# Attention and a gated FFN on one core: where the end keeps its rows of x and gates, and which engine copies and combines at a block change

## The chip, the core and the metric

The kernel runs on one core of a Trainium2 chip. A core has a matmul engine (TensorE, PE in the profile, with its weight loads listed as PEld), VectorE (DVE), ScalarE (ACT), GpSimd (POOL) and SyncE (SP), whose queue issues all the transfers here. Each engine works through its own queue in order; semaphores tie the queues together. [...] The metric is the device time of one execution in microseconds (us); the median of the runs counts.

## The reference

All in fp32, with S = 2048 tokens, D = 576, 32 heads of 18 and F = 4608:

```
xn = layernorm(x)
q, k, v = split(xn @ wqkv)                      # 32 heads of 18
s = softmax(q k^T / sqrt(18)) v  @ wo           # attention block
g = silu( (gelu(xn @ w_gate) * (xn @ w_up)) @ w_down )
out = x + s * g
```

`gelu` is the tanh form. Both branches read the same normalised x; the two results meet in the last line.

## The kernel before

**Tiling.** Tokens come in NB = 4 blocks of TB = 512, the hidden width in 36 slices of 128 for each block, so there are NF = 144 FFN sections. A section n is 27 pairs of matmuls for gate and up (lines 413 to 430, rows `L427`): the 576 input features are nine chunks of 64, and each chunk is multiplied three times, since every fp32 operand is cut into a high part in fp32r and a low part (`wh`, `wl` for the weights, two tiles per chunk group for x). The gate runs on partitions 0 to 63 of the array and up on 64 to 127, so x must lie in both halves: `load_xd` brings it to the lower half and `copy_xd` copies it to the upper, part 0 (high) on ScalarE (`L151`) and part 1 (low) on GpSimd (`L153`). With every new block x is exchanged in this way (`new` in `section`).

After the section `activate` makes the hidden slice h, `sums_a` and `cut_a` build from it the operands `ah` and `al` on GpSimd (`L455`, `L456`, `L462` to `L467`), and every second section `down` multiplies them with the down weights T: 42 matmuls in seven products (`py`, `L538`), each added by VectorE into the accumulator M (`L542`), or copied into it by ScalarE for the first slice of a block (`L540`). The seven products stand for eight (a scheme with sums of sub-blocks), so at the end of a block M's seven parts are combined into four (`combine`, `L553`; the list `COMBINED` gives four times one step on VectorE and one on GpSimd), and `gates` stores the four quarters to `ys` in DRAM.

**Attention** runs between the pairs of the sections. NU = 32 units (a block of queries, four heads) take four sections each; each section has eight slots, a slot being a score pair (`pe`, `L825`, then exp on ScalarE, `L826`) and a maximum pair (`pm`, `L774`, then a reduction on VectorE, `L776`) for the unit after. Values are `acc` (`L842`). When the maxima of a unit are complete, `max_parts` negates them (VectorE), cuts them in two on GpSimd (`L789`, `L790`), turns them on VectorE (`max_turn`, `L795`) and sends them over DRAM (`max_store`, `max_end`) into rows of QT, where the scores of the next unit read them. The last three are hooked between pairs of the following section: pairs 4, 5 and 16.

**Order.** PE and SP follow the program. ScalarE, VectorE and GpSimd are ordered by the framework's planner until the last part, except where an instruction is marked with `keep`: that pins it behind the instruction that the program gives the same engine just before. Hooks (`FF["hooks"]`) name the pair of the next section at which a step is written. In the last part (lines 1063 to 1117) all engines follow the program. Transfers use eight semaphores in turn, and a request waits for the one eight before it.

**The end.** Five gate/up sections are left when attention is over, with three down products. Between them stand 16 groups of 128 tokens, each a `step()`: `split_o` cuts the group's attention output (in KA) into `oh` (ScalarE `L948`, VectorE `L950`) and `ol` (VectorE `L949`); `project_o` multiplies it with wo in 28 matmuls (`po`, `L974`); `gate` makes silu of the stored gate rows by a tanh on ScalarE (`L964`) and a product on VectorE (`L965`); VectorE multiplies this with `po` (`L981`); GpSimd adds x (`L988`; VectorE for the last block), and the group is stored (`L1004`). `load_xy` (`L957`) asks for the rows of x and gates: four x tiles, three gate tiles, two groups ahead. The store of a group is requested one step later than its sum, behind the requests of that step. The cut of a group is queued one group ahead. Scaling the last attention rows (`scale`, `L700`), the loads of gate/up weights (`load_gu`, `L130`) and of T (`t_piece`, `L483`) lie in between.

Of the kernel before, what the change touches and what calls it, by code (L numbers as in the profile page):

```python
# [81 lines left out]
def kernel(ctx: ExitStack, tc: tile.TileContext, x, wqkv, wo, w_gate, w_up, w_down, out):  # L82
# [375 lines left out]
    def sums_a(g, h, eng):  # L458

        if g == 0:  # L460
            FF["h0"] = h
            eng.tensor_tensor(h[:, 2], h[:, 1], h[:, 0], op=ALU.subtract)  # L462
        else:
            h0 = FF.pop("h0")
            eng.tensor_tensor(h[:, 4:6], h0[:, 0:2], h[:, 0:2], op=ALU.add)
            eng.tensor_tensor(h[:, 3], h0[:, 0], h[:, 1], op=ALU.add)
            eng.tensor_tensor(h[:, 2], h[:, 0], h[:, 1], op=ALU.subtract)  # L467
# [61 lines left out]
    def down(b, r, then={}):  # L529
# [3 lines left out]
        for m, (i, k) in PRODUCTS:  # L533
# [5 lines left out]
            if r == 0:  # L539
                nc.scalar.activation(M[:, m], py[:, :, 0:DC], AF.Copy)  # L540
            else:
                nc.vector.tensor_tensor(M[:, m], py[:, :, 0:DC], M[:, m], op=ALU.add)  # L542
# [24 lines left out]
    def section(specials=(), tag="f", slots=False, tail=0):  # L567
# [34 lines left out]
        FF["w"] = nxt  # L602
        FF["act"] = activate(pg, pu, g, n < ATT.stop)
# [19 lines left out]
    def finish():  # L623
# [11 lines left out]
        def behind(what):  # L635
            if (n + 1) % (NR * G) == 0:
                hook(9, what)
            else:
                what()
# [8 lines left out]
        elif (b, r) in FORMED:  # L648
# [10 lines left out]
            else:  # L659
                for k, i in enumerate((2, 9)):  # L660
                    hook(i, lambda k=k: t_piece(r, 2 + k, True))
                behind(lambda: (sums_a(g, h, pool), cut_a(1, h, pool, pool, keep)))
        else:
# [7 lines left out]
            behind(lambda: (sums_a(g, h, pool), cut_a(g, h, pool, pool)))  # L671
# [45 lines left out]
    with tc.tile_pool(name="att", bufs=1, reuse_waits="tile") as att:  # L717
# [64 lines left out]
        def max_neg(u):  # L782
# [6 lines left out]
            keep(nc.gpsimd.tensor_copy(m2[:, :, 0], n2))  # L789
            keep(nc.gpsimd.tensor_tensor(m2[:, :, 1], n2, f(m2)[:, :, 0], op=ALU.subtract))  # L790
# [142 lines left out]
    with tc.tile_pool(name="epi", bufs=1, reuse_waits="tile") as epi:  # L933
        OW = [epi.tile([P, NK, D], F32R, name=name) for name in ("woh", "wol")]
        OP, XY, S2 = {}, {}, {}

        def load_wo():
            nc.gpsimd.memset(f(OW[1])[HR:P, KT, :], 0.0)
            for i, w in enumerate(OW):
                (nc.sync.dma_start(f(w)[:, 0:KT, :], wos[i, 0:R0, :].rearrange("(k p) n -> p k n", p=P)))  # L940
                for a in range(2 - i):
                    (nc.sync.dma_start(f(w)[HR * a:HR * a + HR, KT, :], wos[i, R0:D, :]))

        def split_o(b, j):

            oh, ol = OP[b, j] = [epi.tile([P, k, P], F32R, name=m, bufs=2) for m, k in (("oh", NK), ("ol", KT))]
            raw = f(KA)[:, OTS[b]:OTS[b] + NK, j * P:(j + 1) * P]
            nc.scalar.activation(oh, raw, AF.Copy)  # L948
            nc.vector.tensor_tensor(ol, raw[:, 0:KT], f(oh)[:, 0:KT], op=ALU.subtract)  # L949
            nc.vector.tensor_tensor(oh[HR:P, KT, :], raw[0:HR, KT], f(oh)[0:HR, KT, :], op=ALU.subtract)  # L950

        def load_xy(b, j):

            rows = slice(b * TB + j * P, b * TB + (j + 1) * P)
            XY[b, j] = [epi.tile([P, D], F32, name=m, bufs=n) for m, n in (("xx", 4), ("yy", 3))[0:2 - (b == NB - 1)]]
            for t, a in zip(XY[b, j], (x, ys)):
                nc.sync.dma_start(t, a[rows, :])  # L957

        def gate(b, j):

            if b < NB - 1:
                yy = XY[b, j][1]
                th = epi.tile([P, D], F32, name="th")
                nc.scalar.activation(th, yy, AF.Tanh, scale=0.25)  # L964
                nc.vector.scalar_tensor_tensor(yy, th, 1.0, yy, op0=ALU.add, op1=ALU.mult)  # L965

        def project_o(b, j):

            po = ring("po")
            oh, ol = o = OP.pop((b, j))  # L970
            terms = [(k, x, w) for k in range(KT) for x, w in ((0, 0), (0, 1), (1, 0))] + [(KT, 0, 0), (KT, 0, 1)]
            for c in range(2):
                for m, (k, x, w) in enumerate(terms):
                    nc.tensor.matmul(po[:, c, 0:DC], o[x][:, k, :], OW[w][:, k, DC * c:DC * c + DC], start=(m == 0),  # L974
                                     stop=(m == len(terms) - 1))
            xx = XY[b, j][0]
            gate(b, j)
            if b < NB - 1:
                t = XY[b, j][1]
                t2 = t.rearrange("p (c d) -> p c d", c=2)  # L980
                nc.vector.scalar_tensor_tensor(t2, t2, 0.25, po[:, :, 0:DC], op0=ALU.mult, op1=ALU.mult)  # L981
            else:
                t = epi.tile([P, D], F32, name="last", tag="yy", bufs=3)
                for c in range(2):
                    m = QUARTERS[2 * (j // 2) + c][2]
                    nc.vector.scalar_tensor_tensor(t[:, DC * c:DC * c + DC], FF["M"][:, m, j % 2], 0.25, po[:, c, 0:DC],
# [159 lines left out]
```

## Time and profile before

| | us |
|---|---|
| median of 3 runs | 2613.79 (2611.99 to 2614.08) |
| the profiled execution, its own time | 2614.18 |
| its span, first to last instruction | 2611.7 |
| TensorE busy in it | 2560.9 |
| last matmul ends / last sum ends | 2607.1 / 2608.7 |

A row of a wait list says which engine and line waited for which, how long in total, how often, and the longest. A row of the stages says from and to, the length, then busy time (and count) of PE, PEld, DVE, ACT, POOL, the granted clock of TensorE as a share of full speed, the busy share of the transfer engines and GB/s. A row of the chain says when a piece starts, how long it lasts and what it is; `x` behind it counts instructions. In group rows the shapes stand as output from input, then the count, the busy time, the mean in ns, and the idle time in front with its releaser. Times are us from the first instruction.

### The profile page before, as it was taken

The page shows a single profiled execution, that of the slowest core. Times are in us where ns is not written, and L with a number is a line of the kernel's source. Part 1 is how long each engine was busy: PE and PEld are TensorE (multiplying, and loading weights), DVE is VectorE, ACT ScalarE, POOL GpSimd, SP SyncE. Part 2 cuts the span into 40 slices and gives each one's busy share as a digit, 9 for nine tenths or more (in the row PEclk, how much of TensorE's full clock was granted, in tenths as well). Part 3 has the DMA queues.
Part 4 walks back from the last instruction along what each step waited for, and adds up shares of the span by engine and source line. Part 5 has one row for each costly group of instructions (what it writes and reads, how often), then busy time and mean ns, then how long its engine had stood idle before and what let it go on. Part 6 is the DMA issues. An engine that isn't in the chain of part 4 may idle for free.

```text
span 2611.7 us, 52872 instructions
## 1 busy us (share of the span) xinstructions
PE 2560.9 (98%) x20548; PEld 1858.5 (71%) x20548; DVE 2110.4 (81%) x2386; ACT 1470.5 (56%) x1770; POOL 1607.8 (62%) x1685
## 2 busy tenths in 40 slices
PE   9999999999999999999999999999999999999977
PEld 8887766776766767677766676677766667667777
DVE  6326888888887888988888888888888888886467
ACT  3224366666667655666556666666666556556521
POOL 2215588888888855566666665555556555556652
PEclk9999999999999999999999999999999999999999
DMA  8775355555574566666665666555566655564664
GB/s 268 259 242 141 106 167 159 160 166 162 165 193 159 160 170 163 168 164 163 168 177 163 166 168 158 158 156 157 156 163 200 160 157 156 157 159 133 202 195 141
DMA packets 407880, 442.87 MB, mean 170 GB/s; under 512 B 106700, under 2 KB 286412, under 8 KB 407632
## 3 DMA queue, kind: packets, MB, share of 16 engines
q1 hardware_dynamic: 407632, 439.50, 60.4%
q8 instruction: 163, 2.67, 0.4%
q14 instruction: 85, 0.70, 0.1%
HBM read 344.12 MB, written 95.26 MB: 168 GB/s over the span
## 4 chain that ended last, share of the span: by engine, by line
PE 89%; POOL 4%; DMA 3%; DVE 2%; ACT 1%; issue 1%; SPq 0%; POOLq 0%; DVEq 0%; ACTq 0%
PE pg L427 20%; PE acc L842 17%; PE py L538 14%; PE pu L427 12%; PE pe L825 9%; PE pm L774 9%; PE po L187 7%; PE py L525 1%; DMA raw<-in_B_w_up_dram 1%; PE po L974 1%; DVE mx L776 1%; POOL wl L112 1%; POOL al L456 0%; DMA wol<-wos 0%; POOL wh L110 0%
## 5 line engine op out<-in xcount | busy, mean ns | idle before, releaser
L826 ACT ACTIVATE pT<-pe 128x1024 f32<-128x1024 f32 x1024 | 1047.8, 1026 | 592.2 <-PE pe L825 558.5
L776 DVE TENSOR_REDUCE mx<-pm 128x2 f32<-128x1024 f32 x1024 | 1220.7, 1225 | 182.3 <-PE pm L774 171.2
L427 PE MATMUL pu<-xd,wh 64*128 64x512 f32 x2538 | 927.9, 397 | 5.4 <-POOL xd L153 3.8
L427 PE MATMUL pg<-xd,wh 64*128 64x512 f32 x2538 | 927.1, 397 | 1.9 <-ACT t L440 1.9
L427 PEld LDWEIGHTS pg<-xd,wh 64*128 64x128 f32 x2538 | 468.8, 185 | 109.7 <-issue 59.6
L427 PE MATMUL pg<-xd,wl 64*128 64x512 f32 x1269 | 496.7, 391 | 1.2 <-POOL wl L117 1.2
L427 PE MATMUL pu<-xd,wl 64*128 64x512 f32 x1269 | 496.6, 391 | 0.0
L427 PEld LDWEIGHTS pu<-xd,wh 64*128 64x128 f32 x2538 | 468.7, 185 | 35.4 <-POOL xd L153 5.1
L110 POOL TENSOR_SCALAR wh<-raw 128x384 fp32r<-128x384 f32 x402 | 215.8, 538 | 437.5 <-PE pu L427 321.5
L842 PE MATMUL acc<-pT,VS 128*32 128x512 f32 x4096 | 466.0, 595 | 0.0
L112 POOL TENSOR_TENSOR wl<-raw,wh 128x384 fp32r<-128x384 f32 x402 | 413.0, 1030 | 28.5
L825 PE MATMUL pe<-QT,KA 64*128 64x512 f32 x2048 | 416.2, 394 | 8.6 <-DVE mx L776 6.9
L774 PE MATMUL pm<-KA,QT 64*128 64x512 f32 x2048 | 418.1, 393 | 4.5 <-DVE mx L776 2.8
L538 PE MATMUL py<-T,ah 128*128 128x288 f32 x1876 | 383.1, 300 | 4.7 <-DVE yy L981 4.7
L542 DVE TENSOR_TENSOR M<-py,M 128x576 f32<-128x576 f32 x448 | 339.2, 757 | 32.1 <-PE py L538 18.6
L538 PEld LDWEIGHTS py<-T,ah 128*128 128x128 f32 x1876 | 300.4, 189 | 58.9 <-issue 58.5
L456 POOL TENSOR_TENSOR al<-h,ah 128x512 fp32r<-128x512 f32 (+1 forms) x142 | 292.2, 2058 | 52.6 <-ACT ah L453 41.1
L842 PEld LDWEIGHTS acc<-pT,VS 128*32 128x32 f32 x4096 | 120.1, 109 | 276.6 <-issue 229.7
L825 PEld LDWEIGHTS pe<-QT,KA 64*128 64x128 f32 x2048 | 194.1, 184 | 122.1 <-DVE mx L776 30.1
L538 PE MATMUL py<-T,al 128*128 128x288 f32 x938 | 276.9, 295 | 0.0
L427 PEld LDWEIGHTS pg<-xd,wl 64*128 64x128 f32 x1269 | 234.5, 185 | 29.3 <-POOL wl L117 2.0
L427 PEld LDWEIGHTS pu<-xd,wl 64*128 64x128 f32 x1269 | 234.4, 185 | 14.4
(153 smaller groups left out, 2929.1 us busy)
## 6 DMA issues: line engine op xcount, KB each, us to landing
T<-ts SPq DMA_DIRECT2D x98, 576.0 KB
KA<-qk SPq DMA_DIRECT2D x768, 72.0 KB
T<-ts SPq DMA_DIRECT2D x98, 432.0 KB
raw<-in_B_w_gate_dram SPq DMA_DIRECT2D x144, 288.0 KB
raw<-in_B_w_up_dram SPq DMA_DIRECT2D x144, 288.0 KB
ts<-T SPq DMA_DIRECT2D x36, 576.0 KB
VS<-vs SPq DMA_DIRECT2D x128, 152.0 KB
qk<-t SPq DMA_DIRECT2D x72, 256.0 KB
```

The lines of the kernel that those rows point to most:

```text
L110: first = nc.gpsimd.tensor_scalar(hi, raw, 1.0, 1.0, op0=ALU.mult, op1=ALU.mult)
L112: keep(nc.gpsimd.tensor_tensor(lo, raw, f(hi), op=ALU.subtract))
L187: nc.tensor.matmul(o, st, m, start=(i == 0), stop=(i == len(terms) - 1))
L427: nc.tensor.matmul(o, w[1 + wp][k][rr, c, :], xd[k][xp][rr, c, :], start=(i == 0), stop=(i == len(terms) - 1))
L456: keep(two.tensor_tensor(lo, raw, f(hi), op=ALU.subtract))
L538: nc.tensor.matmul(py[:, t, 0:DC], h[:, i, tt], T[:, w, k], start=n == 0, stop=n == 2)
L542: nc.vector.tensor_tensor(M[:, m], py[:, :, 0:DC], M[:, m], op=ALU.add)
L774: nc.tensor.matmul(pm[:, a], QS[u, r][rr, t * P:(t + 1) * P], KS[(u * NA + c) % KB][r][rr, :], start=True, stop=True)
L776: return nc.vector.tensor_reduce(MX[u][:, 2 * r:2 * r + 2, t, c], pm, axis=AX.X, op=ALU.max)
L825: nc.tensor.matmul(pe[:, a], KS[(u * NA + c) % KB][r][rr, t * P:(t + 1) * P], QS[u, r][rr, :], start=True, stop=True)
L826: nc.scalar.activation(PT[u, kt][:, 2 * r:2 * r + 2, :], pe, AF.Exp, scale=SCALE)
L842: nc.tensor.matmul(ACC[u][32 * a:32 * a + 32, :], VS[(u * NA + c) % VB][:, v:v + 32], pt[:, a, :], start=first, stop=last, skip_group_chec ...
```

## The change

It has two parts.

In the last part of the kernel the tiles for rows become seven for x (three, and four in the space of the scaled rows) and four for gates. `load_xy` is asked for four groups ahead, right behind the group's own store, which is requested as soon as its sum is queued. All sums of x are on VectorE. The cut and the gate of group k+2 are queued behind the sum of group k, so cuts are two groups ahead. The reciprocal's store and the first cut stand earlier, the second cut stands in front of the end of the second section, the gate/up weights are requested one by one at named places (the last of them after two groups), and both scaled-row steps come ahead of the sums.

At block changes the copy of the first x group's high part is put ahead of `activate`, the others go to hooks of the next section (pairs 2, 4, 6 and 9, 11, 13), and the sums in `sums_a` are pinned with `keep` where they are hooked there. `COMBINED` runs wholly on GpSimd after the second and third block. The first slice's copy into M is on VectorE for the second block. `max_turn`, `max_store` and `max_end` move to pairs 8, 9 and 18; for the first unit they go to 0, 1 and 14, and its cut in two is done by VectorE.

The renaming of helpers and of `ALU.add` is left out here.

```diff
-    def sums_a(g, h, eng):
+    def sums_a(g, h, eng, keep=lambda i: i):
...
+            keep(eng.tensor_tensor(h[:, 4:6], h0[:, 0:2], h[:, 0:2], op=ADD))
+            keep(eng.tensor_tensor(h[:, 3], h0[:, 0], h[:, 1], op=ADD))
+            keep(eng.tensor_tensor(h[:, 2], h[:, 0], h[:, 1], op=SUB))
...
             if r == 0:
-                nc.scalar.activation(M[:, m], py[:, :, 0:DC], AF.Copy)
+                if b == 1:
+                    nc.vector.tensor_copy(M[:, m], py[:, :, 0:DC])
+                else:
+                    nc.scalar.activation(M[:, m], py[:, :, 0:DC], AF.Copy)
...
-            for i, one, two in COMBINED:
-                FF["hooks"].setdefault(i, []).append(lambda a=one, b=two: (combine(nc.vector, *a), combine(nc.gpsimd, *b)))
+            one = nc.vector if b == 0 else nc.gpsimd
+            for i, p, q in COMBINED:
+                FF["hooks"].setdefault(i, []).append(lambda p=p, q=q: (combine(one, *p), combine(nc.gpsimd, *q)))
...
+        if new:
+            copy_xd(xd[0], 0, keep)
         FF["act"] = activate(pg, pu, g, n < ATT.stop)
...
-            for k in range(2):
-                copy_xd(xd[k], 0, keep)
-            for i in range(XG):
-                FF["hooks"].setdefault(4 + 4 * i, []).append(lambda i=i: copy_xd(xd[NG - 1], 0, keep, i))
+            for k in range(1, NG):
+                for i in range(XG):
+                    FF["hooks"].setdefault(7 * k + 2 * i - 5, []).append(lambda k=k, i=i: copy_xd(xd[k], 0, keep, i))
...
-            keep(nc.gpsimd.tensor_copy(m2[:, :, 0], n2))
-            keep(nc.gpsimd.tensor_tensor(m2[:, :, 1], n2, f(m2)[:, :, 0], op=ALU.subtract))
+            eng = nc.gpsimd if u > 0 else nc.vector
+            keep(eng.tensor_copy(m2[:, :, 0], n2))
+            keep(eng.tensor_tensor(m2[:, :, 1], n2, f(m2)[:, :, 0], op=SUB))
...
-            for i, part in ((4, max_turn), (5, max_store), (16, max_end)):
+            for i, part in ((8, max_turn), (9, max_store), (18, max_end)) if u > 0 else ((0, max_turn), (1, max_store), (14, max_end)):
...
+        XX = [epi.tile([P, D], F32, name=f"xx{i}") for i in range(3)]
+        YY = [epi.tile([P, D], F32, name=f"yy{i}") for i in range(4)]
...
+        def load_xy(k):
+            if k < len(groups):
+                nc.sync.dma_start(XX[k % len(XX)], x[rows(k), :])
+                if groups[k][0] < NB - 1:
+                    nc.sync.dma_start(YY[k % 4], ys[rows(k), :])
...
+        def multiply(k, po):
...
+            vec.tensor_tensor(xx, xx, t, op=ADD)
+            nc.sync.dma_start(out[rows(k), :], xx)
 
         def step():
             nonlocal n
+            multiply(n, project(n))
+            split_o(n + 2)
+            gate(n + 2)
+            load_xy(n + 4)
+            for t in pieces[:2]:
+                t()
+            del pieces[:2]
             n += 1
-            ready()
-            project_o(*groups[n - 1])
-            if n + 1 < len(groups):
-                load_xy(*groups[n + 1])
-            for p in pieces[:2]:
-                p()
-            del pieces[:2]
-            if n > 1:
-                store()
...
+        load_raw(first + 2)
         h, end = last_section("f")
-        ready()
+        todo.pop("rec")[0]()
+        split_o(0)
         end()
         sums_a(1, h, vec)
         cut_a(1, h, act, vec)
         load_wo()
-        load_xy(*groups[0])
-        todo.pop("rec")[0]()
-        load_xy(*groups[1])
         load_scale(rest[0])
+        load_xy(0)
+        load_xy(1)
+        load_raw(first + 3)
         h, end = last_section("ring")
+        split_o(1)
         end()
+        scale(rest[0])
+        store_scale(rest.pop(0))
+        if rest:
+            load_scale(rest[0])
+        load_xy(2)
         h1, end = last_section("f")
-        scaled_rows()
-        FF["down"].clear()
         last_down(0)
         end()
+        gate(0)
+        while rest:
+            scale(rest[0])
+            store_scale(rest.pop(0))
...
+        gate(1)
+        for m in ("rawd", "tsum"):
+            t = ffn.tile([P, 2, D], F32, name="xxs", tag=m)
+            XX.extend((t[:, 0], t[:, 1]))
+        load_xy(3)
+        for k in range(2):
+            step()
+        load_raw(first + 4)
+        for k in range(2):
             step()
```

More of the change, by code (lines that the diff above doesn't have):

```diff
@@ L967, in project_o @@
[L967 to L981, printed above, removed]
+                    nc.sync.dma_start(f(w)[HR * a:HR * a + HR, KT, :], wos[i, R0:D, :])
@@ L988, in project_o @@
[L988 to L1004 removed]
+                    vec.scalar_tensor_tensor(t2[:, c], FF["M"][:, m, j % 2], 0.25, po[:, c, 0:DC], op0=ALU.mult, op1=ALU.mult)
@@ L1085 @@
         cut_a(1, h1, pool, pool)
-        step()
-        while rest:
-            scaled_rows()
-        for k in range(3):
+        gate(1)
[7 more added lines that the diff above has]
+        for k in range(2):
             step()
```

126 lines of the change are left out of this document (61 added, 65 removed).

## The prediction

> **What bounds the kernel now.** I read the page first, then busy time by stage, then the waits of each engine over the end, then the chain of work that ended last.
>
> ```profile
> span 2611.7 us, 52872 instructions
> PE 2560.9 (98%) x20548; PEld 1858.5 (71%) x20548; DVE 2110.4 (81%) x2386; ACT 1470.5 (56%) x1770; POOL 1607.8 (62%) x1685
> ```
>
> The stages, with PE, PEld, DVE, ACT, POOL busy, then the granted clock:
>
> ```profile
> 2500.00:2550.00 50.00, 36.15 (x236) 32.83 (x235) 28.04 (x35) 8.36 (x13) 29.61 (x24) 0.90 0.70 221
> 2550.00:2580.00 30.00, 25.97 (x188) 23.98 (x187) 19.23 (x26) 7.75 (x11) 6.57 (x4) 0.94 0.54 176
> 2580.00:2612.00 32.00, 22.18 (x149) 21.18 (x148) 23.79 (x33) 4.73 (x7) 8.85 (x5) 0.94 0.26 89
> ```
>
> TensorE is the bound nearly everywhere: 2611.7 - 2560.9 = 50.8 us idle in all, and 27.7 us of that lie in these last 112 us (4.6 of them behind the last matmul). What could be won is there, and the waits say by what it is held (window 2490 to 2612; total us, times, longest):
>
> ```profile
> PE po L974 <- DVE ol L949: 9.5, 7, 3.3
> PE po L974 <- ACT oh L948: 7.5, 3, 3.1
> PE py L538 <- DVE yy L981: 4.7, 1, 4.7
> ACT th L964 <- DMA yy<-ys: 36.0, 7, 12.2
> SPq L957 <- DMA out_dram<-xx: 55.1, 12, 8.2
> POOL wh L110 <- DMA raw<-in_B_w_up_dram: 16.0, 1, 16.0
> ```
>
> TensorE waits 21.7 us for operands that ScalarE and VectorE cut (oh, ol) or for PSUM that they free. Behind those, ScalarE waits 36 us for rows of gates, and the queue that asks for rows (SP) waits 55 us for earlier stores to land. The chain shows the loop closing:
>
> ```profile
> 2519.75 1.40 POOL xx L988
> ...
> 2524.95 4.17 DMA out_dram<-xx
> ...
> 2534.51 4.45 DMA yy<-ys
> ...
> 2539.82 0.77 DVE yy L965
> 2540.68 0.77 DVE yy L981
> 2541.58 6.57 PE py L538 x30
> 2548.15 7.43 PE po L974 x56
> ...
> 2562.03 0.61 ACT h L1047
> ...
> 2568.25 1.21 DVE al L456
> 2569.66 0.69 DVE ol L949
> ...
> 2575.64 3.18 PE py L538 x24
> ...
> 2588.41 1.96 DVE yy L965
> ...
> 2594.41 12.69 PE po L974 x82
> ...
> 2607.97 0.76 DVE xx L988
> ```
>
> A sum on GpSimd, a store, a load that needs the stored tile or the row tile the sum read, a tanh, and only then matmuls: about one such round per group instead of one matmul block. A group's 28 matmuls are 7.43 / 2 = 3.72 us.
>
> **The change at the end, step by step.** The durations of the steps (window 2490 to 2612, mean ns; then min/median/max for L950):
>
> ```profile
> L988 POOL TENSOR_TENSOR xx<-xx,yy 128x576 f32<-128x576 f32 x12 | 20.0, 1670 | 42.7 <-DVE yy L981 42.7
> L965 DVE SCALAR_TENSOR_TENSOR yy<-th,yy 128x576 f32<-128x576 f32 x12 | 12.4, 1030 | 18.2 <-ACT th L964 18.0
> L542 DVE TENSOR_TENSOR M<-py,M 128x576 f32<-128x576 f32 x16 | 12.0, 755 | 2.6 <-PE py L538 2.4
> L988 DVE TENSOR_TENSOR xx<-xx,last 128x576 f32<-128x576 f32 x4 | 3.0, 759 | 0.1
> L950 DVE TENSOR_TENSOR oh<-KA,oh x16: 284/866/1404, 2476.1 to 2603.4; 64x128 fp32r<-64x128 f32 x16
> ```
>
> *Sums from GpSimd to VectorE*: 12 x 1670 = 20.0 us leave GpSimd, 12 x 759 = 9.1 us come to VectorE. A group on VectorE is then multiply 0.77 + sum 0.76 + ol 0.69 + second oh 0.28 + gate 0.77 = 3.27 us (the uncovered rows above and below): under TensorE's 3.72, so hidden as long as GpSimd is quiet. While GpSimd computes, the two-input instructions of VectorE stretch (L950 from 284 to 1404, L965 from 770 to 1960). With four of the five at the 1.4 of the slowest L950 a group is 4 x 1.4 + 0.77 = 6.4 us. Between 3.3 and 6.4 I take 5.2 for the first groups, since GpSimd has work through all of them.
>
> [...]
>
> *Rows*: seven x tiles and four gate tiles for four and three, asked for four groups ahead. Requests now follow the sum of the same group, and the gate of group k is taken two groups after its request, about 2 x 3.72 = 7.4 us, against a landing of 4.45 us in the chain. Its bounds: fully hidden, or behind the larger transfers in the same queue, where a store took 8.2 us (the SP row), so 0.8 us late in each of some six groups, 5 us. I take hidden. *Stores at once*: the SP queue now stands on the sum of a group, with loads, T pieces, KA loads and one load of raw behind it; all these are wanted at least two groups later. Loading the last raw weights later (after two groups) is hidden: their section is some 30 us off. Two requests get a new wait in front of everything behind them: the reciprocal's store, now ahead of wo, and the first x row in the tiles that the scaled rows used, which stands on their stores. wo is read only after two more sections and a down product, that row three groups later: both 0, and without that cover at most the wait itself, one reciprocal or one landing.
>
> *Splits two groups ahead*: oh and ol of group k+2 are queued right after group k's sum. So the two groups after the last section no longer stand behind al on ScalarE and VectorE.
>
> By stretches of TensorE, the time before and then the steps laid out by hand:
>
> ```profile
> 2513.91 0.37 PE L974 MATMUL po<-woh,oh 128*128 128x288 f32 x1 [1.10 <-DVE yy L981]
> ```
>
> 1. To the end of the last section but one, 2513.91 - 1.10 = 2512.8: split_o(1) moves in front of VectorE's work on the section before, about 1 us, and the sums of groups 0 to 2 fall in the time in which GpSimd still cuts (it waited 16 us for raw, and that load is behind the same transfers as before). 5.2 - 3.72 = 1.5 us on one group: **+2.4** (0 to +6).
> 2. From there to the start of the blocks at 2548.15, 35.3 us: three groups 11.2, a down product of 42 matmuls at the 3.18 / 24 of a later row, 5.6, and 1.8 for the sums, splits and gates queued ahead of its M additions: 18.6. **-16.7** (-10 to -18).
> 3. Two groups and the last section, to 2562.0: as before, **0**.
> 4. From 2562.0 to the last down product at 2575.6, 13.6 us: two groups 7.4 and 0.4 for al, which still takes from 2562.03 to 2569.46: **-5.8** (-3 to -6.2).
> 5. From there to the last matmul, 2607.1, 31.5 us: VectorE has two groups' multiply, sum, split waiting behind al (5.9 us) before the first M addition, so TensorE stops twice (2.6 and 1.7 us), and four group tails follow. By hand 31: **-0.5** (-6 to +4).
>
> Sum 2.4 - 16.7 - 5.8 - 0.5 = -20.6. Behind the last sum (2607.97 + 0.76) 3 us remain as they are.
>
> A second weighing: what a stop costs beside itself. At a block change the granted clock (the first number behind POOL's) is at half right after a stop:
>
> ```profile
> 1351.50 0.50 PE L427 MATMUL pu<-xd,wh 64*128 64x512 f32 x1 [2.42 <-POOL xd L153]
> 1352.20:1355.60 3.40, 3.40 (x20) 2.65 (x18) 2.06 (x2) 1.02 (x1) 3.16 (x6) 0.50 1.00 310
> ```
>
> [...] Here a gap of 2.42 us was enough. [...]
>
> **The change at block changes and at the first unit.** Waits of TensorE from 330 to 2460, then one of 200 to 330, then M's sums in the section after a change:
>
> ```profile
> PE pe L825 <- DVE mx L776: 6.9, 13, 1.0
> PE pu L427 <- POOL xd L153: 3.8, 2, 2.4
> ...
> PE pm L774 <- DVE mx L776: 2.6, 1, 2.6
> ...
> L553 POOL TENSOR_TENSOR M<-M x4: 1427/1435/1914, 1367.7 to 1372.2; 128x576 f32<-128x576 f32 x4
> L553 DVE TENSOR_TENSOR M<-M x4: 741/746/1291, 1372.1 to 1380.3; 128x576 f32<-128x576 f32 x4
> ```
>
> *x copies ahead of sums*: 3.8 us in two changes, and 1.7 for the half clock after one; if the planner obeys, 5.5; the new edges pin the sums only behind the GpSimd instruction before them, so I take **-3.5** (-5.5 to +2, a copy waiting for its load). *Combinations on GpSimd at two changes*: 4 x 1435 = 5.7 us more on GpSimd, 4 x 746 less on VectorE, whose L776 holds TensorE: **-2** of the 6.9 (-3 to +1); stores of ys wait for them, the next writer of M comes a section later. *First unit*: m2 on VectorE, two instructions of some 0.2 us instead of a 2.6 us wait: **-2.5** (-4.3 with the half clock, to 0). *Copies of M on VectorE* (755 each) at one change: hidden, VectorE has only those there; without that cover 7 x 0.1. *max_turn later*: in a steady unit it unblocks VectorE; taken 0.
>
> Sum -8. Against the profiled execution's own 2614.18: 2614.18 - 20.6 - 8 = 2585.6; it stands 0.4 above the median 2613.79. I say 2586.
>
> **The rivals.** (a) *The planner leaves block changes as they are*: the end alone, 2593. For it: the soft edges; against: the xd copies and L776 waits are plain. (b) *VectorE becomes the bound of the end*: every group at 5.2 for 3.72 in stretches 2 and 4, 5 x 1.5 = 7.4, stretch 1 at +6 and stretch 5 at +4: 2586 + 7.4 + 3.6 + 4.5 = 2601.5. For it: nine more microseconds there; against: GpSimd is empty after its cuts. (c) *The rows are still late*: 5 us, and two stops with half clock, 3.4: 2594; with (a) 2602. That is also how the change would fail to do what it says. (d) *Slower*: every unit's maxima now leave at pair 9 and land after pair 18 instead of 16:
>
> ```profile
> L813 SPq DMA_DIRECT2D QT<-mxT x2: 229/242/254, 1392.5 to 1392.8; - x2
> ...
> 1404.07 0.40 PE L825 MATMUL pe<-QT,KA 64*128 64x512 f32 x2
> ```
>
> The transfer is asked for at 1392.77 and first read at 1404.07, 11 us with some 4 for landing, and two of 27 pairs of a 14 us section are 1 us. It decides only where the turn is held some 6 us more, say by the GpSimd work that now runs in a fixed order in front of m2. The price would be a stop in each of 31 units, between the 1.0 us of the longest L776 wait and the 2.4 us of the longest for xd; at 1.4, the other one for xd, 2586 + 31 x 1.4 = 2629. From 28 / 31 = 0.9 us a unit on it decides.
>
> **How the numbers follow.** The forecast, 2578 to 2593 by itself, has 0.52; (a) 0.15; (b) 0.13; (c) 0.08; (d) or another order of the planner that costs as much 0.08; the rest, 0.04, is no change, where gains at the end are given back in other sections. A difference under 0.2%, 5.2 us, is about what a measurement of this kernel can't tell from none. So faster 0.88, within 0.04, slower 0.08. The range reaches down to 2576, where stretches 1 and 2 and the block changes give nearly their full bounds, and up to 2604, past (b) and (c) with (a). It leaves out (d) and the joint ends of the bounds.
>
> **What would show it.** Each step has its row in the changed profile:
> - The wait of th for yy (36.0 us) falls under 8, and the wait of SP for out_dram (55.1) under 20; if they stay, (c).
> - GpSimd has no L988 form, VectorE has 16 of about 760 to 1900 ns; stops of the first four groups on ol sum to 2 to 4 us.
> - No wait of L974 for oh over 1 us; the largest stops at the end stand in the last down product, on VectorE's M additions and multiplies.
> - The last matmul is some 28 us earlier, and the clock over the last 112 us is above 0.97.
> - At block changes the wait for xd (3.8) is gone and that for mx falls to about 5; the 2.6 us stop of L774 before 330 is gone.
> - From 330 to 2460 TensorE's waits don't grow; if they do by over 10 us, (d).
>
> I am wrong if VectorE, not TensorE, is the engine without gaps in stretches 2 and 4, if gates still land late behind T and KA, or if the planner, which orders three engines anew, opens stops in sections that the change doesn't touch.

## The result and the profile after

The changed kernel takes 2595.99 us (median of 4 runs, 2595.73 to 2598.46) beside 2613.93 for the kernel before in the same session: a ratio of 0.9933, with a 95% interval of 0.9915 to 0.995. It is faster, and inside the range of the prediction, but 10 us above the time that was called likeliest. The profiled execution's own time is 2595.73. The page, then the stages of the end as before (from and to, length, PE, PEld, DVE, ACT, POOL, granted clock, share of the transfer engines, GB/s):

```profile
span 2593.9 us, 52857 instructions
PE 2554.1 (98%) x20548; PEld 1847.5 (71%) x20548; DVE 2111.7 (81%) x2399; ACT 1468.6 (57%) x1769; POOL 1599.7 (62%) x1679
```

```profile
2476.00:2500.00 24.00, 20.12 (x140) 19.46 (x139) 19.36 (x23) 4.63 (x7) 15.49 (x15) 0.95 0.61 153
2500.00:2550.00 50.00, 42.40 (x303) 38.46 (x301) 34.98 (x46) 10.43 (x17) 12.54 (x11) 0.92 0.80 265
2550.00:2580.00 30.00, 26.65 (x176) 25.43 (x173) 25.87 (x35) 8.03 (x12) 7.09 (x4) 0.89 0.27 95
```

The clock was to be above 0.97 over the last 112 us; it is 0.92 there, and 0.89 to 0.95 in these stages. TensorE's stops over 0.3 us in the end (timeline, start of the matmul behind the stop, the stop in brackets; one more, of 0.43, stands at 2477.53):

```profile
2496.84 0.40 PE L991 MATMUL po<-woh,ol 128*128 128x288 f32 x1 [3.30 <-DVE ol L973]
...
2517.88 0.40 PE L991 MATMUL po<-woh,ol 128*128 128x288 f32 x1 [1.47 <-DVE ol L973]
...
2528.28 0.82 PE L538 MATMUL py<-T,ah 128*128 128x288 f32 x2 [4.68 <-DVE yy L1000]
2531.35 0.85 PE L538 MATMUL py<-T,ah 128*128 128x288 f32 x2 [1.28 <-DVE M L545]
...
2562.05 0.53 PE L538 MATMUL py<-T,ah 128*128 128x288 f32 x2 [2.16 <-DVE yy L1000]
2564.44 0.85 PE L538 MATMUL py<-T,ah 128*128 128x288 f32 x2 [0.90 <-DVE M L545]
```

The first four are most of the missing gain: 10.7 us, and half clock behind two of them (3.41 us from 2497.5 and 6.83 from 2528.3). The waits (2480 to 2594; total, times, longest) and the chain of work over the same stretch say what is late:

```profile
ACT th L982 <- DMA yy<-ys: 28.0, 6, 8.4
...
SPq L1006 <- DMA KA<-on: 3.1, 1, 3.1
```

```profile
2499.29 10.31 DMA KA<-on
2509.67 1.35 SPq L1006
2511.53 8.04 DMA yy<-ys
2519.66 0.70 ACT th L982
2520.38 1.44 DVE yy L983
2521.82 0.68 DVE yy L1000
...
2523.83 1.21 DVE ol L973
2525.07 0.58 DVE oh L974
2525.68 1.79 DVE yy L983
2527.47 0.68 DVE yy L1000
```

Rows of gates are still late: 28.0 us of waiting, where under 8 was to be seen. But it is no longer a store and a row tile that hold them: the queue's waits for stores are down from 55.1 us to under 2. Two other things do. The first is the landing itself. Group 5's row was requested at 2501.63, without a wait, and the tanh that reads it could start only at 2511.58, 9.95 us later, beside KA, T and the last raw weights (rows of SP and of ScalarE):

```profile
2501.63 0.57 SPq L964 DMA_DIRECT2D yy<-ys  x1
...
2511.58 0.69 ACT L982 ACTIVATE th<-yy 128x576 f32<-128x576 f32 x1 [8.44 <-DMA yy<-ys]
```

The second is the queue. The new columns of KA (requested at 2499.29) land after 10.31 us. The store of group 2, whose sum was done at 2504.7, is the eighth request counted from them, so behind the requests for the raw weights it waits another 3.1 us for that landing and goes out at 2509.67; the requests of group 6's rows stand behind it, and take 8.04 us among T and the last raw weights. Then VectorE, which in its order has the gate of group 6 ahead of the multiply of group 5, does late work with GpSimd beside it (gates of 1.44 and 1.79 us for 0.76).

By the prediction's stretches (us, from the first matmul of the first of the three down products to the last matmul, read from TensorE's rows in each trace; the versions are those of the experiments below):

| | to the end of the last section but one | to the start of the blocks | two groups, last section | to the last down product | to the last matmul | sum |
|---|---|---|---|---|---|---|
| before | 28.5 | 35.2 | 13.9 | 13.6 | 31.6 | 122.8 |
| predicted | 30.9 | 18.6 | 13.9 | 7.8 | 31.1 | 102.3 |
| changed kernel | 33.2 | 27.9 | 13.9 | 7.5 | 31.7 | 114.1 |
| e_raw | 33.2 | 24.1 | 13.9 | 7.5 | 31.6 | 110.3 |
| e_gate | 29.5 | 27.8 | 13.9 | 7.5 | 32.5 | 111.2 |
| e_rows | 31.4 | 24.2 | 13.9 | 7.5 | 31.7 | 108.6 |
| e_pool | 28.6 | 43.3 | 13.9 | 7.5 | 32.7 | 125.9 |
| e_defer | 33.1 | 27.1 | 13.9 | 7.5 | 31.2 | 112.7 |
| e_best1 | 29.0 | 25.0 | 13.9 | 7.5 | 32.5 | 108.0 |
| e_best2 | 29.0 | 17.4 | 13.9 | 7.5 | 32.0 | 99.8 |

The changed kernel once more, on another chip, gave 113.7. Ahead of the end, the first matmul of each of the 72 down products is set against the same one of another trace, and where the difference jumps, time was won or lost in between. Before against after: -2.43 at the first unit; +0.50 and +1.67 behind the first and the second block change, then -1.17, -1.16 and -2.01 one or two products later; -2.10 after the third; -1.16, -0.50 and -0.57 between 2130 and 2340; -9.6 in all from the first product on, which itself comes 0.58 later, so -9.1 where the end begins. Such a jump differs by up to 1.3 us between two executions of the changed kernel (behind the second change, where half clock lasts 6.83 us in one and 3.41 in the other), and by 1.8 between it and e_pool, whose instructions are the same up to the end (half clock from 746.4).

### The profile page after: what moved, and what is told of

It is laid out like the page before. It is cut to its first block, busy times and chain, and to the rows that moved or that the text cites. A ratio compares the mean times of both kernels' runs of the same rounds, so it can differ in the third digit from the quotient of the medians.

```text
span 2593.9 us, 52857 instructions
## 1 busy us (share of the span) xinstructions
PE 2554.1 (98%) x20548; PEld 1847.5 (71%) x20548; DVE 2111.7 (81%) x2399; ACT 1468.6 (57%) x1769; POOL 1599.7 (62%) x1679
## 4 chain that ended last, share of the span: by engine, by line
PE 92%; DVE 2%; DMA 2%; POOL 1%; ACT 1%; issue 1%; SPq 1%; POOLq 0%; DVEq 0%; ACTq 0%
PE pg L427 27%; PE acc L848 17%; PE py L538 14%; PE pe L831 9%; PE pm L779 9%; PE po L187 7%; PE pu L427 7%; PE py L525 1%; PE po L991 1%; DMA raw<-in_B_w_up_dram 0%; DMA wol<-wos 0%; DVE mx L781 0%; DMA KA<-on 0%; PE pt L248 0%; DMA yy<-ys 0%
## 5 line engine op out<-in xcount | busy, mean ns | idle before, releaser
L112 POOL TENSOR_TENSOR wl<-raw,wh 128x384 fp32r<-128x384 f32 x402 | 413.4, 1031 | 28.6
L545 DVE TENSOR_TENSOR M<-py,M 128x576 f32<-128x576 f32 x448 | 338.8, 758 | 31.2 <-PE py L538 18.5
L456 POOL TENSOR_TENSOR al<-h,ah 128x512 fp32r<-128x512 f32 (+1 forms) x142 | 292.8, 2062 | 52.6 <-ACT ah L453 42.5
```

Of the source, the lines that this page charges most:

```text
L112: keep(nc.gpsimd.tensor_tensor(lo, raw, f(hi), op=ALU.subtract))
L456: keep(two.tensor_tensor(lo, raw, f(hi), op=ALU.subtract))
```

## The experiments

The ratios are to the kernel before, with 95% intervals. An interval is some 4.5 us to each side, so single steps are read from the traces and the ratio is the test on the whole.

**The changed kernel again.**

> The changed kernel itself, beside the next three on the same chip, so that a difference of two of them is not one of chips. Its ratio to the kernel before was 0.9933 with an interval of 0.9915 to 0.995; expected 0.992 to 0.994, and in its trace 113 to 115 us from the down product to the last matmul.

0.9933 (0.9915 to 0.9951): no difference between the chips in the ratio.

**The main part alone.** Everything ahead of the last part's tile pool as in the changed kernel, and from there on (helpers and sequence) the kernel before.

> The end of the kernel before, with everything that the change does ahead of the end (x copies, combinations, first unit, later turn of the maxima). Theory 1 (the two parts add up): the traces put 9.1 us of the gain ahead of the end and 8.6 in it, so 2613.9 - 9.1 = 2604.8, 2603 to 2607, with the old end's waits back (ScalarE for rows of gates some 36 us, TensorE for oh some 7). Rival (the end wins only because it starts earlier or with other buffers): under 2601 or over 2609.

0.9949 (0.9932 to 0.9965), which is 9 to 18 us and holds both theories. The traces decide: the jumps ahead of the end are those of the changed kernel (-8.7 at 2336 for -9.0), and the end is as long as before or longer (125.1 for 122.8), with 38.3 us of waiting for gates. The parts add up.

**The copies of x, by force.**

```diff
-            keep(nc.gpsimd.tensor_copy(x[1][HR:P, i], x[1][0:HR, i]))
+            keep(FF.setdefault("copy", [None]).__setitem__(0, nc.gpsimd.tensor_copy(x[1][HR:P, i], x[1][0:HR, i])) or FF["copy"][0])
...
-            h0 = FF.pop("h0")
-            keep(eng.tensor_tensor(h[:, 4:6], h0[:, 0:2], h[:, 0:2], op=ADD))
+            one, h0 = eng.tensor_tensor(h[:, 4:6], FF["h0"][:, 0:2], h[:, 0:2], op=ADD), FF.pop("h0")
+            keep("copy" in FF and after(one, FF.pop("copy")[0], "sums behind the copies of x") or one)
```

The first line remembers the last copy; the last one makes the first sum behind a block change depend on it (`after`).

> The changed kernel, with one edge added: the first sum of h on GpSimd at a block change depends on the last copy of x, so the copies really stand ahead of the sums (in the changed kernel the sums still ran between the first and the second tile's copies, 1340.3 to 1347.3, while the second tile had landed by 1340 or so). Theory 1 (my step's idea was right, the soft edges did not carry it): the 3.60 us stop at 1344.42 and its half clock to 1354.0 go, and the 1.27 us stop at 743.64: 4 to 7 us, 2589 to 2592. Rival (the stop moves): ah and al then come 3 to 4 us later, the down product that follows waits for them, and the time is 2595 to 2598.

0.9913 (0.9898 to 0.9928). What the change had left undone stands in GpSimd's timeline of the changed kernel at the second block change; `x3` are the copies of one x group, L465 to L456 the sums and cuts:

```profile
1337.56 1.72 POOL L153 CAST xd<-xd 64x512 fp32r<-64x512 f32 x3
1340.29 1.29 POOL L465 TENSOR_TENSOR h<-h,h 128x512 f32<-128x512 f32 x1 [1.01 <-DVE h L444]
...
1344.41 2.88 POOL L456 TENSOR_TENSOR al<-h,ah 128x1280 fp32r<-128x1280 f32 x1
1347.36 1.73 POOL L153 CAST xd<-xd 64x512 fp32r<-64x512 f32 x3
```

```profile
1348.02 0.79 PE L427 MATMUL pu<-xd,wh 64*128 64x512 f32 x1 [3.60 <-POOL xd L153]
```

The sums run between the copies exactly as before the change. With the edge, the copies come first. My expectation was wrong in one point: the second group had not landed by 1340, GpSimd waits for it until 1344.61. The same view of the version with the edge:

```profile
1344.61 1.73 POOL L153 CAST xd<-xd 64x512 fp32r<-64x512 f32 x3 [1.28 <-DMA xd<-xhs]
...
1348.78 1.73 POOL L153 CAST xd<-xd 64x512 fp32r<-64x512 f32 x3
1350.59 1.29 POOL L464 TENSOR_TENSOR h<-h,h 128x512 f32<-128x512 f32 x1
```

The stop of 3.60 and its half clock (6.83 us from 1347.2) are gone, and the next products are 4.4 us earlier (3.1 against the second execution of the changed kernel). At the first change the next product is 1.75 earlier, but the one after is 3.16 later. There GpSimd has forming of T to do as well, and the later sums push the cut of the maxima in front of which VectorE waits:

```profile
779.69 0.20 POOL L795 CAST m<-nm 128x16 fp32r<-128x16 f32 x1
```

```profile
782.16 0.50 PE L831 MATMUL pe<-QT,KA 64*128 64x512 f32 x2 [1.63 <-DVE mx L781]
```

(776.60 for the former in the changed kernel.) So both theories held, each at one change: the order is worth 3.1 to 4.4 us where GpSimd has slack, and costs 1.4 to 1.6 where it is the late engine.

**Combinations back on VectorE.**

```diff
-            one = nc.vector if b == 0 else nc.gpsimd
+            one = nc.vector
```

> The changed kernel with one of each pair of combinations back on VectorE at all three block changes, as before. My step (4 of 746 ns off VectorE at two changes are worth 2 us in all) says about 2 us slower; the milestones of the two traces, -2.0 after each of the last two changes, say 4. Rival (GpSimd is the late engine there, as at the first change, where its sums now push the maxima): 0 to 3 us faster.

0.9947 (0.9928 to 0.9966), and jumps of +2.20 and +2.18 behind the last two changes, against the second execution of the changed kernel: 4.4 us, the milestones' figure, twice my step. Over all that stands ahead of the end it is less, 2.4 and 3.5 us against the two executions, and the medians on the same chip are 3.65 apart (2603.00 and 2599.35).

**The turn of the maxima at its old pairs.**

```diff
-            ... ((8, max_turn), (9, max_store), (18, max_end)) if u > 0 else ...
+            ... ((4, max_turn), (5, max_store), (16, max_end)) if u > 0 else ...
```

> The changed kernel with the turn of the maxima, their store and their load back at pairs 4, 5 and 16 of the section, as before, for all units but the first. My step: 0. The traces put 2.2 us of gain on the sections from 2131 to 2336 that nothing else touches: if they are the turn's, the time is 2 to 4 us higher than the changed kernel's, with VectorE's waits for GpSimd's m2 back at 5 us or more. Rival (d), the later turn makes the maxima late: 2 us or more lower.

0.9929 (0.9912 to 0.9947): the times show no difference. The trace shows one: by 2330 the products are 2.5 to 3.8 us later, set against the two executions of the changed kernel, in jumps of 0.4 to 1.3. And two waits from 330 to 2460, which in the changed kernel are 0.9 and 1.9 us, are back:

```profile
DVE mt L801 <- POOL m L796: 6.3, 6, 1.4
PE pe L831 <- DVE mx L781: 5.8, 9, 1.1
```

The later turn lets VectorE reduce on instead of waiting for GpSimd's cut. It is no loss, as rival (d) would have it; how much it gains the times leave open.

**The end: transfers only.** T's four pieces follow `gate(0)` at once, and KA's columns for block 2 follow the first four steps.

```diff
         gate(0)
+        for t in pieces:
+            t()
+        del pieces[:]
...
-            if b < 2 and j == TB // P - 1:
+            if b == 1 and j == TB // P - 1:
                 load_o(b + 2)
...
         for k in range(2):
             step()
+        load_o(2)
         h, end = last_section("ring")
```

> The changed kernel with transfers moved only: all four T pieces (2 MB) asked for right after the down product that frees T, while the queue would otherwise stand until 2492.6 for a scaled row, and KA's new columns (1.2 MB) after the four groups instead of after the second; the last raw weights, VectorE's and GpSimd's order as in the changed kernel. Theory A (rows of gates late, behind T and KA and behind the queue's wait for the transfer eight requests before): gates of groups 3 to 7 land in time, the waits of th for yy fall from 28.0 to under 15 us, the stops of 1.47 and 4.68 us at 2516.41 and 2523.61 shrink to under 2 in sum and their half clock goes: from the down product to the last matmul 105 to 109 us for 114.1, and the time 5 to 9 lower than the changed kernel's. The stop of 3.30 at 2493.54, on group 2's row, stays. Theory B (VectorE stretched by GpSimd): GpSimd's work is the same, so 0 to 3.

0.9902 (0.9881 to 0.9922), and the end is 5.5 us shorter. The wait of th for yy is 14.4 us as theory A had it, but the stops were not under 2 us:

```profile
2518.14 0.40 PE L991 MATMUL po<-woh,ol 128*128 128x288 f32 x1 [2.01 <-DVE ol L973]
...
2527.61 0.84 PE L538 MATMUL py<-T,ah 128*128 128x288 f32 x2 [3.38 <-DVE M L545]
```

The 4.68 us stop on a late multiply has become one of 3.38 on the M additions: from 2508 to 2558 the chain of this version holds no transfer, VectorE's own instructions in their order have taken the place.

**The end: the last raw weights later.** Asked for after the first of the three groups behind the section, and split behind the sums that follow the down product.

```diff
-        load_raw(first + 4)
         for k in range(2):
             step()
         h, end = last_section("ring")
         end()
-        for k in range(3):
+        step()
+        load_raw(first + 4)
+        for k in range(2):
             step()
         last_down(1)
         sums_a(0, h, pool)
         cut_a(0, h, pool, pool)
+        FF["w"] = FF["raw"].pop(first + 4)
+        for k in range(NG):
+            split_gu(FF["w"], k)
```

> The changed kernel, with the last load of raw weights asked for after the first of the three groups behind the last section but one, and GpSimd's split of it after the last down product but one's sums, instead of ahead of both. This takes two transfers of some 11.5 us landing out of the way of the rows of groups 5 to 7 and takes 5.4 us of GpSimd out of 2517.9 to 2523.3. Theory A (rows late) and theory B (VectorE stretched by GpSimd) both say that the stops of 1.47 and 4.68 us at 2516.41 and 2523.61 go, with half clock 3.4: 6 to 9 us, 2587 to 2590. They differ in the rows: A says the wait of th for yy falls from 28.0 us to under 18, B says that the second form of the gate for groups 6 and 7 falls from 1.44 and 1.79 us to 0.76 while yy still lands late. Rival C (the order of the work, gate of group k+2 ahead of the multiply of k+1, whatever the rows do): under 3 us gained.

0.9911 (0.9896 to 0.9926), the end 3.8 us shorter, less than either theory said. The stop of 4.68 on a late multiply has become one of 3.39 on the M additions; 3.30 and 1.47 stay. The gates of groups 6 and 7 are at 0.76 us while the wait for yy stays at 25.2, as theory B had it. But that sum hides the one row that counts: ScalarE's wait for group 6's row falls from 4.71 to 1.25 us, and VectorE no longer waits for its gate. So the row came earlier and the gates became shorter in the same version, and it can't tell A from B.

**The end: the gate one group later in the order.**

```diff
             split_o(n + 2)
-            gate(n + 2)
+            gate(n + 1)
...
-        gate(1)
```

> The changed kernel, with the gate of group k+1 instead of k+2 taken at the end of a group's step, so that a row of gates may land 3.7 us later before anything stands behind it; transfers and GpSimd unchanged. Theory A (rows late block VectorE and ScalarE in their order): the stops of 3.30, 1.47 and 4.68 us at 2493.54, 2516.41 and 2523.61 shrink to under 3 in sum: 5 to 9 us gained, 2587 to 2591. Theory B (VectorE is stretched while GpSimd computes): the same work in another order, 2594 to 2597.

0.991 (0.9895 to 0.9924), the end 2.9 us shorter: neither A's 5 nor B's nothing in the trace. The stop of 3.30 falls to 1.05 and that of 1.47 is gone, but the down product after them still stops for 4.77 and then 3.59 us: VectorE reaches it sooner, and stands there for group 6's row all the same.

**The end: sums of x back on GpSimd.**

```diff
-            vec.tensor_tensor(xx, xx, t, op=ADD)
+            (pool if b < NB - 1 else vec).tensor_tensor(xx, xx, t, op=ADD)
```

> The changed kernel with the 12 sums of x for the first three blocks back on GpSimd, everything else as changed. [...] Rival (b), VectorE is the bound of the end: 9 us less on VectorE, the end is 3 to 6 us shorter.

0.9959 (0.9944 to 0.9974), the end 11.8 us longer, where the rival had it 3 to 6 shorter. It is not GpSimd's time: in its program's order the sums stand behind the split of the last raw weights, and that waits for its transfer, so stores and with them rows come late (wait of th for yy 44.5 us). GpSimd's row in front of that split:

```profile
2530.06 0.51 POOL L110 TENSOR_SCALAR wh<-raw 128x384 fp32r<-128x384 f32 x1 [14.60 <-DMA raw<-in_B_w_up_dram]
```

In the first stretch, though, this version is 4.6 us faster than the changed kernel (28.6 for 33.2): there the sums on VectorE do cost, as rival (b) said.

**The end: tails behind the M additions.** At the last two down products VectorE does the M additions straight behind the group's multiply (in the last one behind its split too); the group's sum, split and gate follow.

```diff
-            vec.tensor_tensor(xx, xx, t, op=ADD)
+
+        def add(k):
+            xx = XX[k % len(XX)]
+            vec.tensor_tensor(xx, xx, YY[k % 4], op=ADD)
...
-        def step():
+        def step(then=None):
             nonlocal n
             multiply(n, project(n))
-            split_o(n + 2)
+            if then and n > 8:
+                split_o(n + 2)
+            if then:
+                then()
+            add(n)
+            if not then or n < 8:
+                split_o(n + 2)
...
-        last_down(1)
+        step(lambda: last_down(1))
```

(`last_down(2, ...)` is called in the same way.)

> The changed kernel with one thing moved on VectorE at the last two down products: the M additions come straight behind the multiply of the group ahead of them (in the last one behind its split too), and that group's sum, split and gate behind the M additions. Theory C (order: the stops of TensorE in front of the third product are the tail of a group on VectorE, 3 to 5 us with the stretching by GpSimd): the stops of 1.28 at 2530.06, 2.16 at 2559.88 and 0.90 at 2563.54 shrink to under 1.5 in sum and the half clock after them goes: 3 to 6 us; the 4.68 us stop stays, since the multiply itself is late there. Rival (VectorE has the work all the same, and later stops take it back): under 1.5 us.

0.9916 (0.9893 to 0.994), the end 1.4 us shorter in the trace: alone it is next to nothing there, as the rival had it. The medians on the same chip say more, 2595.18 for 2599.35, but these runs spread over 6.6 us, and the two profiled executions took 2596.49 and 2596.60. The 1.28 and 0.90 us stops are gone, 2.16 and 4.68 stay, and a new one of 1.63 comes behind the last down product.

**Together.** First e_xdep's edge (not at the first change), e_raw, e_gate and e_rows:

> Five edits together: the edge of e_xdep, but not at the first block change, the last raw weights late as in e_raw, the gate one group ahead as in e_gate, and the transfers of e_rows. By the single runs the block change gives 4.4 us, and if rows were the whole cause the end falls from 114.1 to 103 to 107 us, with only the stops in front of the M additions left: 2596 - 4.4 - 9 = 2582.6, 2579 to 2587. If VectorE's work and the M additions are the bound instead, the end stays over 109 and the time over 2587.

0.9877 (0.9861 to 0.9894); the end is 108.0, hardly under e_rows alone. What is left stands in VectorE's timeline of this version: a multiply, and the four instructions of the rest of its step ahead of the first M addition, for which TensorE waits 3.41 us:

```profile
2516.60 0.75 DVE L1000 SCALAR_TENSOR_TENSOR yy<-yy,po 128x576 f32<-128x576 f32 x1
2517.39 0.76 DVE L1005 TENSOR_TENSOR xxs<-xxs,yy 128x576 f32<-128x576 f32 x1
2518.07 1.10 DVE L973 TENSOR_TENSOR ol<-KA,oh 128x512 fp32r<-128x512 f32 x1
2519.20 1.23 DVE L974 TENSOR_TENSOR oh<-KA,oh 64x128 fp32r<-64x128 f32 x1
2520.46 0.76 DVE L983 SCALAR_TENSOR_TENSOR yy<-th,yy 128x576 f32<-128x576 f32 x1
2521.14 1.42 DVE L545 TENSOR_TENSOR M<-py,M 128x576 f32<-128x576 f32 x2
```

Then the deferred tails as well:

> The five edits of the first combined version and the deferred tails. In the combined version's trace the stops that are left are 3.41 us in the last down product but one, where VectorE has sum, ol, oh and gate (0.76, 1.10, 1.23, 0.76) between the multiply and the first M addition, and 2.38 and 2.05 in the last, each with half clock behind it. By theory C these go nearly all: 4 to 7 us below the combined version, which was 0.9877 of the kernel before, so 0.985 to 0.9865. If later stops take it back, 0.987 to 0.988.

0.9864 (0.9846 to 0.9881), 2580.23 us where the changed kernel took 2599.35 on the same chip: 19 us less, the fastest of all, and at the edge of what theory C said. In the trace the end is 99.8 us, 8.2 less than without the deferred tails and six times what they gave alone; by the ratios it is 3.4 us, with intervals that overlap, so the size rests on the traces. TensorE's stops over 0.65 us in the end are two:

```profile
2545.78 0.50 PE L538 MATMUL py<-T,ah 128*128 128x288 f32 x2 [2.37 <-DVE yy L1000]
...
2561.73 0.40 PE L991 MATMUL po<-woh,ol 128*128 128x288 f32 x1 [1.68 <-DVE ol L973]
```

And it isn't that VectorE's instructions became shorter. The gates and the cuts of the end by groups, in the changed kernel and then in this version (busy, mean ns):

```profile
L973 DVE TENSOR_TENSOR ol<-KA,oh 128x512 fp32r<-128x512 f32 x14 | 12.7, 906 | 0.0
L983 DVE SCALAR_TENSOR_TENSOR yy<-th,yy 128x576 f32<-128x576 f32 x12 | 12.1, 1009 | 10.4 <-ACT th L982 10.2
```

```profile
L983 DVE SCALAR_TENSOR_TENSOR yy<-th,yy 128x576 f32<-128x576 f32 x12 | 12.4, 1030 | 1.5 <-ACT th L982 1.2
L973 DVE TENSOR_TENSOR ol<-KA,oh 128x512 fp32r<-128x512 f32 x14 | 11.7, 839 | 0.0
```

The gates are as long as they were and the cuts 7% shorter. So theory B explains little of it; what counts is which instructions stand between a multiply and TensorE's next need, and whether a late row stands among them. No run takes GpSimd's work away alone, so what the stretching costs by itself stays open.

## Why the prediction was right, and where it was wrong

The range held, the direction was right, and rival (c), the rows still late, at 2594 (worked out as 5 us and two stops with half clock, each half of the 3.40 us at 0.50 at 1352.20), describes what happened better than the forecast at 2586. Half of rival (a) is true as well: at the block changes GpSimd's copies did not move.

- **Stretch 2, -16.7 predicted, -7.3 measured.** This is the step that failed, and it is the sentence "I take hidden" on the rows. It set 7.4 us of lead against one landing of 4.45; here group 5's row came after 9.95 us and group 6's after 8.04. Its bound, 5 us, read the 8.2 us of SP's row as the time of a store. That row is the longest of twelve waits of the queue, 55.1 us in all, so it showed already that the queue itself stands: a request waits for the one eight before it, and KA's new columns, T and the raw weights are among these eight. "All these are wanted at least two groups later" was true of the transfers and false of the requests behind them: group 6's row was asked for 6.8 us after the sum it followed. The matmul terms were sound: without the 1.8 us of tails they are 16.8, and e_best2, with the tails behind the M additions, needs 17.4. But it takes transfers, gate and tails together.
- **"1.8 for the sums, splits and gates queued ahead of its M additions"** in the same stretch was too small: 3.85 us stand between a multiply and the first M addition in e_best1 (0.76 + 1.10 + 1.23 + 0.76), and with three PSUM slots TensorE gets only three products done meanwhile, the third from 2517.51, once the multiply has freed its slot. The largest stops were to stand in the last down product; in the changed kernel they stand in the one before it.
- **Stretch 1, +2.4 predicted, +4.7 measured.** The mechanism was named (sums of groups 0 to 2 while GpSimd cuts); e_pool, e_rows and e_best1 show that late rows and the sums' place share it. **Stretches 3 and 4** came as laid out (0, and -6.1 for -5.8). **Stretch 5** too (+0.1 for -0.5): two stops of 2.16 and 0.90 for the 2.6 and 1.7 forecast, with 6.83 us of half clock behind them, for which the sum has no term; the chain runs over VectorE there, 2566.3 to 2577.9.
- **Sums on VectorE:** e_pool (+11.8) shows that in this program's order they belong there, because on GpSimd they stand behind a split that waits for a load and so hold the stores. What a sum costs by its length on GpSimd is not what it shows, and GpSimd in another order was not run. VectorE's L950 took 284 to 288 ns in the kernel before where GpSimd was idle and up to 1404 beside its work; what holds it up there, no run shows.
- **x copies, -3.5 predicted, +2.2 measured** in one execution and +0.7 in the other (the jumps behind the two changes). The doubt stood in the step ("pin the sums only behind the GpSimd instruction before them") and should have decided it. With a real edge the second change gains 2.7 us against the kernel before, and the first loses 0.7.
- **Combinations, -2 predicted, -4.4 by e_comb's jumps in two places,** -3.65 by its time. I had taken it out of one wait, 6.9 us for mx, which fell to 1.9. **Later turn, 0 predicted,** a gain of 2.5 to 3.8 by e_turn's trace alone; VectorE's waits for m2 went with it. **First unit, -2.5 predicted, -2.43 measured,** but not as laid out: 1.4 us of the 2.6 us stop stay, and the half clock behind it (3.41 us from 311.1) is gone, which the -2.5 left out and only its bound of -4.3 counted. That the number fits is luck. Of the M copies on VectorE I have no run alone, nor of what gives -1.17 and -1.16 behind the first change.
- **One reading was too wide:** the chain of the kernel before shows a store and then a load in front of matmuls once in the end (2524.95 to 2538.96), not once per group.

The parts ahead of the end summed to -9.1 for -8 by errors of opposite sign; the end to -8.7 for -20.6.

## What to carry to other kernels

Price a request by the queue, not by its own transfer: where a request waits for an earlier one, a large load holds what follows it until it has landed, however late its own data is wanted (here a store that was ready at 2504.7 went out at 2509.67). When several waits of one loop end close together, undoing one shows the next: the three edits to rows and gates gave 5.5, 3.8 and 2.9 us alone and 6.1 together, and the deferred tails gave 1.4 alone and 8.2 behind those three. So a small gain from one edit is no proof that its cause is small; that the total, 14.3, is near the sum of the single gains, 13.6, is chance. And an order that has to hold needs an edge to the very instruction it should follow; look into the changed trace whether it does.

## What the hardware showed that I had not expected

Whether half clock followed a stop of TensorE was not a matter of its length alone: it came behind the stop of 2.16 us in the changed kernel and did not behind one of 2.38 us at 2495.80 in e_rows. Windows of 3.4 us around the two:

```profile
2559.00:2562.40 3.40, 1.24 (x9) 1.03 (x9) 3.32 (x6) 0.00 (x0) 0.00 (x0) 1.00 0.52 173
2562.40:2565.80 3.40, 2.50 (x11) 2.15 (x10) 3.27 (x6) 0.00 (x0) 0.00 (x0) 0.50 0.54 174
2565.80:2569.20 3.40, 3.40 (x16) 3.40 (x16) 2.85 (x4) 0.00 (x0) 0.62 (x1) 0.50 0.00 0
2569.20:2572.60 3.40, 3.40 (x27) 3.40 (x27) 3.33 (x4) 0.00 (x0) 3.21 (x2) 1.00 0.02 5
```

```profile
2493.50:2496.90 3.40, 2.30 (x18) 2.06 (x16) 3.37 (x4) 0.55 (x1) 3.23 (x4) 1.00 0.55 210
2496.90:2500.30 3.40, 2.12 (x16) 2.12 (x17) 2.49 (x2) 0.00 (x0) 3.40 (x4) 1.00 0.27 73
2500.30:2503.70 3.40, 3.40 (x28) 2.93 (x29) 0.65 (x1) 1.31 (x2) 3.23 (x3) 1.00 1.01 334
```

In the first, TensorE is busy for 1.24 of 3.40 us in one window, and the clock is at half in the next; that one, with 2.50, is followed by another at half. In the second the longer stop falls on two windows with 2.30 and 2.12, and the clock stays full. In the changed kernel, up to the last matmul, half clock begins at 1347.2, 2497.5, 2528.3 and 2562.4 and lasts 3.413 us at the second and 6.827 at the others, by the clock's records in the trace; the beginnings are 337, 9 and 10 times 3.413 us apart. Laid on each trace's own grid of 3.413 us, the windows of the kernels before and after from 250 us on fit one picture: at full clock, the eleven with 1.25 us or less of busy TensorE were each followed by half clock, and none of the others, with 1.84 us or more, was; at half clock, the four with 1.84 to 2.65 us were followed by another at half, the ten with 3.04 us or more by full clock. So the 2.42 us of my row is no bound, and where a stop falls on the grid can decide over a window at half clock, an estimated 3.41 / 2 = 1.7 us where TensorE is the bound.
